# Attention into an MLP block on one core: per-head loads for the first two batches, key bias inside the score matmul, weights cast by DMA, 1/std at the output

## The chip, the core and the metric

The kernel runs on one core of one Trainium2 chip. The engines are TensorE (PE; its weight loads are shown as PEld), VectorE (DVE), ScalarE (ACT), GpSimd (POOL) and SyncE (SP, which here only issues DMAs). The metric is the device time of one execution in microseconds.

## The reference

Attention over 8 batches of 8 heads, 576 tokens, head size 64, with a bias from a running sum; then, on the concatenated heads (512 wide), a normalization, two matmuls with a ReLU between them, and a residual.

```python
scores = scale * np.matmul(q, k.transpose(0, 1, 3, 2))        # scale = 1/8
cum = np.cumsum(np.maximum(s, 0.0), axis=-1)
bias = -(cum[:, :, :, None] - cum[:, :, None, :])
scores = np.where(causal, -1000000000.0, scores + np.minimum(bias, 0.0))
attn = softmax(scores)
x = concat_heads(np.matmul(attn, v))                          # (8, 576, 512)
xn = (x - mu) / np.sqrt(var + 1e-06) * g_ln
out = x + np.maximum(xn @ w_ch1, 0.0) @ w_ch2                 # 512 -> 2048 -> 512
```

Inputs and the output are float32; the kernel's matmuls are bfloat16 with float32 sums.

## The kernel before

**Tiles.** A batch's 576 tokens are four full blocks of 128 and a tail of 64. Scores are held transposed, with keys on the partitions; only the causal part is computed, five key blocks with 576, 448, 320, 192 and 64 query columns, 1600 in all. The tile `aug` holds a batch's q and k for all heads in bfloat16, tokens on the partitions. In column 64 q carries minus the running sum and k carries a one, so the score matmul (65 rows deep) subtracts the query's sum. The key's sum is added by the bias operand of the exp, one exp for each key block (`score_exp`, L186). GpSimd then zeroes the upper triangle of the diagonal blocks. `values` (L207) multiplies with v, whose 65th column of ones gives the denominator, and DVE divides.

**Transposes.** q and k must stand with the head size on the partitions (`qkT`). For batches 0 and 1 PE transposes them head by head (`t_pe`, L150). For batches 2 to 7 DMA transposes do, one for each token block of all heads, issued by SP (`t_dma`, L157). The normalized activations are transposed by DMA too (`x_t`, L293; for chunk 0 by PE).

**The MLP.** Each batch's four full token blocks are one chunk. The tails of four batches make a half-size chunk each (chunks 8 and 9). `chunk_units` (L321) puts a chunk's work into a list of units of four 128 x 128 x 512 matmuls: 16 units up (each followed by a ReLU, ACT and DVE by turns) and 16 down (every fourth followed by the residual add); a tail chunk has 16 in all. The loop over the 64 heads takes units off this list, `n_units` a head (4 unless the table says otherwise), and sets them between the score matmuls of head g, its exps, and the values of head g-1. So the order on every engine is the order in which this loop issues work.

**Loads.** Everything comes as float32 into a staging ring of eight tiles (`stage`), loaded by SP for a token block of all eight heads (for batch 0 of four heads, `half`, L366), and is cast on DVE, ACT or POOL. A load waits until `casts` has freed a tile. The first weight is loaded in the same way in sixteen pieces and scaled by the gain in the cast (`cast_w1`, L136); the second goes through four casting DMAs issued by POOL (L500).

**Normalization.** `norm` (L263): DVE takes mean and variance, POOL computes (variance + eps) to the power -0.5, DVE subtracts and scales, a transpose and the up-matmuls follow.

**The start.** Batch 0's heads run without units. Then, at g = 8, chunk 0 is normalized, 11 units run, and batch 1 is cast and begins with one unit a head. At g = 16 ten units stand between the transposes of batch 2.

## Time and profile before

| | before |
|---|---|
| median of 3 runs | 460.45 us (458.38 to 460.86) |
| the profiled execution | 456.99 us, span 455.3 us |
| PE busy | 365.8 us (80%), 2741 matmuls |
| DVE busy | 204.1 us (45%) |
| ACT busy | 189.4 us (42%), of it exps 127.8 and 21.3 us |
| POOL busy | 148.2 us (33%) |
| mean granted PE clock | 0.908 |
| DMA moved | 64.61 MB, mean 142 GB/s; SP's queue 61.1% of the 16 engines |

A row of a busy group reads: line, engine, operation, what is written and from what, shapes, count; then busy time and mean ns of one; then the engine's idle time just before these instructions and what ended most of it. A timeline row reads: start and duration in us, engine, line, operation, tiles, count, and in brackets the idle time before it with its releaser. `SPq` rows are SP's DMA issues.

### The profile page before, as it was taken

The numbers are of one execution on the slowest core, as the hardware profiler recorded it, in microseconds if no ns is written. First come the engines' busy times: TensorE is split into PE (matmuls) and PEld (weight loads), VectorE is DVE, ScalarE is ACT, GpSimd is POOL, SyncE is SP. The second block draws the span as 40 slices with busy tenths as digits, with TensorE's granted clock in tenths as the row PEclk, the third lists the DMA queues.
The fourth block names the chain that finished last, engine by engine and source line by source line (L and its number), as shares of the span: only waits on it lengthen the run. The fifth ranks groups of instructions, "written<-read, shape, count | busy, mean of one in ns | idle before, by whom it ended". The sixth has DMA issues, their size and how long they took to land.

```text
span 455.3 us, 7530 instructions
## 1 busy us (share of the span) xinstructions
PE 365.8 (80%) x2741; PEld 198.7 (44%) x2741; DVE 204.1 (45%) x462; ACT 189.4 (42%) x408; POOL 148.2 (33%) x307
## 2 busy tenths in 40 slices
PE   1982745894074999699919999968999999999995
PEld 1751313551032555355517545534555455444472
DVE  7557233571042455353734374317436544723231
ACT  2753521760051654365405574525555644203020
POOL 4333312452143344443633365315433222100000
PEclk9996685999575999899968999979999999999999
DMA  7990699729968993999498929992992111320112
GB/s 169 205 326 20 96 212 200 150 36 225 215 144 178 207 199 96 194 209 214 112 208 177 233 65 169 219 249 48 193 205 72 31 46 48 61 80 24 48 46 46
DMA packets 202277, 64.61 MB, mean 142 GB/s; under 512 B 193472, under 2 KB 195520, under 8 KB 202240
## 3 DMA queue, kind: packets, MB, share of 16 engines
q1 hardware_dynamic: 196352, 55.22, 61.1%
q10 hardware_dynamic: 3776, 6.82, 4.4%
q0 software_dynamic: 2112, 2.10, 2.9%
q8 instruction: 21, 0.34, 0.3%
q14 instruction: 16, 0.13, 0.1%
HBM read 36.85 MB, written 9.44 MB: 102 GB/s over the span
## 4 chain that ended last, share of the span: by engine, by line
PE 57%; DVE 13%; DMA 8%; POOL 5%; issue 5%; SPq 4%; ACT 2%; DVEq 0%; POOLq 0%; ACTq 0%
PE py L345 22%; PE ph L334 22%; PE s L174 6%; PE pot L216 4%; SPq L102 3%; DVE xn L287 3%; DMA qkT<-aug 3%; DVE stats L261 3%; POOL rstd L270 2%; DVE hT L319 2%; SPq L158 2%; DVE x L226 1%; DMA xnT<-xn 1%; ACT e L192 1%; DVE yo L351 1%
## 5 line engine op out<-in xcount | busy, mean ns | idle before, releaser
L192 ACT ACTIVATE e<-s,cumk 128x576 bf16<-128x576 f32 (+3 forms) x256 | 127.8, 582 | 112.4 <-PE s L174 97.7
L334 PE MATMUL ph<-xnT,w_bf 128*128 128x512 bf16 x512 | 128.0, 396 | 14.9 <-DMA xnT<-xn 9.7
L345 PE MATMUL py<-w_bf,hT 128*128 128x512 bf16 x576 | 135.2, 382 | 0.0
L199 POOL TENSOR_SCALAR_AFFINE_SELECT e<-e 128x512 bf16<-128x512 bf16 (+1 forms) x128 | 59.5, 488 | 167.8 <-issue 93.5
L334 PEld LDWEIGHTS <-w_bf 128*128 128x128 bf16 x640 | 61.5, 102 | 82.0 <-issue 24.1
L317 ACT ACTIVATE hT<-ph 128x512 bf16<-128x512 f32 x72 | 43.4, 603 | 121.8 <-PE ph L334 115.1
L319 DVE TENSOR_SCALAR hT<-ph 128x512 bf16<-128x512 f32 x72 | 49.4, 689 | 74.6 <-PE ph L334 73.3
L345 PEld LDWEIGHTS <-hT 128*128 128x128 bf16 x576 | 53.3, 98 | 57.1 <-issue 1.7
L174 PE MATMUL s<-qkT 65*128 65x512 bf16 (+4 forms) x320 | 60.2, 320 | 21.4 <-DMA qkT<-aug 21.2
L174 PEld LDWEIGHTS <-qkT 65*128 65x128 bf16 x384 | 34.7, 105 | 62.5 <-issue 29.8
L225 DVE RECIPROCAL rinv<-pot 128x5 f32<-128x5 f32 x64 | 12.2, 191 | 91.9 <-PE pot L216 90.1
L118 POOL CAST aug<-st 128x512 bf16<-128x512 f32 (+3 forms) x65 | 39.4, 630 | 21.9 <-DMA st<-in_k_dram 21.9
L216 PEld LDWEIGHTS <-e 128*128 128x128 bf16 x960 | 39.7, 101 | 14.5 <-POOL e L199 3.0
L216 PE MATMUL pot<-v_bf,e 128*128 128x65 bf16 x960 | 42.7, 199 | 2.6 <-POOL e L199 1.8
L351 DVE TENSOR_TENSOR yo<-py,x 128x512 f32<-128x512 f32 x32 | 22.1, 690 | 26.4 <-PE py L345 25.2
L226 DVE TENSOR_TENSOR x<-pot,rinv 128x320 f32<-128x320 f32 x64 | 31.5, 492 | 2.2
L154 PE MATMUL pt<-ident,aug 128*128 128x128 bf16 x160 | 17.4, 269 | 14.1 <-DVE aug L132 11.3
L287 DVE TENSOR_SCALAR xn<-x,mv,rstd 128x512 bf16<-128x512 f32 x30 | 21.1, 740 | 16.3 <-POOL rstd L270 15.1
L334 PE MATMUL ph<-xnT_tail,w_bf 128*128 128x256 bf16 x128 | 16.5, 290 | 9.5 <-DMA xnT_tail<-xn 9.5
L118 POOL CAST v_bf<-st 128x512 bf16<-128x512 f32 (+1 forms) x35 | 20.6, 613 | 10.4 <-DMA st<-in_v_dram 10.4
L261 DVE BATCH_NORM_STATS2 stats<-x 128x6 f32<-128x256 f32 (+2 forms) x68 | 23.2, 396 | 0.0
L192 ACT ACTIVATE e<-pot,cumk 128x64 bf16<-128x64 f32 x64 | 21.3, 332 | 1.0 <-PE pot L174 1.0
(51 smaller groups left out, 128.0 us busy)
## 6 DMA issues: line engine op xcount, KB each, us to landing
st<-in_k_dram SPq DMA_DIRECT2D x28, 256.0 KB, 4.6
st<-in_v_dram SPq DMA_DIRECT2D x28, 256.0 KB, 4.1
st<-in_q_dram SPq DMA_DIRECT2D x24, 256.0 KB, 4.4
out_dram<-yo ACTq DMA_DIRECT2D x24, 256.0 KB, 3.6
hT<-in_moe_w_ch_dram SPq DMA_DIRECT2D x8, 256.0 KB, 5.7
st<-in_moe_w_ch_dram SPq DMA_DIRECT2D x8, 256.0 KB, 5.5
w_bf<-in_moe_w_ch_dram POOLq DMA_DIRECT2D x4, 512.0 KB, 10.1
out_dram<-yo SPq DMA_DIRECT2D x8, 256.0 KB, 2.0
```

Source lines behind the costliest of these rows:

```text
L118: nc.gpsimd.tensor_copy(out=o, in_=i)
L174: nc.tensor.matmul(o, lhsT=qkT[b][0:D1, H + h, kb * P : (kb + 1) * P], rhs=qkT[b][0:D1, h, lo:hi], start=True, stop=True,)
L192: nc.scalar.activation(out=e[:, kb * S : kb * S + w], in_=srcs[kb], func=ACT.Exp, bias=cumk[:, kb, g : g + 1], scale=scale,)
L199: nc.gpsimd.affine_select(out=o, in_=o, compare_op=ALU.is_ge, fill=0.0, base=0, pattern=[[0, n], [1, P]] if n > 1 else [[1, P]], channel_m ...
L216: nc.tensor.matmul(pot[:, t * D1 : (t + 1) * D1], lhsT=e[:, c : c + P], rhs=v_bfs[b % 2][:, kb, h, :], start=(kb == 0), stop=(kb == t),)
L226: nc.vector.tensor_tensor(out=xs[b][:, :, h * D : (h + 1) * D], in0=pv[:, :, 0:D], in1=rv.to_broadcast([P, NT, D]), op=ALU.mult,)
L261: nc.vector.bn_stats(out=sts[c, a][:, part, :], in_=x_of(c, a)[:, lo:hi])
L287: nc.vector.tensor_scalar(out=xn[:, j, :], in0=x_of(c, a), scalar1=mv[:, j, 0:1], scalar2=rstd[:, j : j + 1], op0=ALU.subtract, op1=ALU.mult,)
L317: nc.scalar.activation(out=o, in_=i, func=ACT.Relu)
L319: nc.vector.tensor_scalar_max(out=o, in0=i, scalar1=0.0)
L334: nc.tensor.matmul(ph[:, j * tok : (j + 1) * tok], lhsT=w1_bf[:, kd, fb * P : (fb + 1) * P], rhs=xnT[c][:, :, kd, :], start=(kd == 0), sto ...
L345: nc.tensor.matmul(st["py"], lhsT=st["h"][:, fb, a * P : (a + 1) * P], rhs=w2_bf[:, fb, :], start=(fb == 0), stop=(fb == FB - 1),)
```

## The change

1. **Loads of batches 0 and 1.** Each head's q, k and v are loaded apart, 128 partitions x 4 token blocks x 64, straight into fixed tiles (`homes`: the ring, now ten tiles, and two of the three x buffers). The tails of all heads come in one load for each of q, k, v. `cast_head` casts a head's five blocks at once, q on DVE, k and v on POOL. Batch 1 is issued at heads 5 to 7.
2. **Key bias in the matmul.** The running sum times 8 is split into three bfloat16 parts (`split`), which stand in k's columns 65 to 67 against ones in q. The score matmul is 68 rows deep, and the exps need no bias, so the blocks that lie next to each other in PSUM go in one exp: 1024, 512 and 64 columns, three a head. `shift` writes both parts; from batch 2 on POOL does it, not DVE.
3. **Weights.** Both go through casting DMAs on POOL, the first at heads 2 to 5 and the second at heads 9 to 12.
4. **1/std at the output.** The gain multiplies x minus mean. The factor 1/std is left out of xn (ReLU lets a positive factor through) and multiplies the second matmul's result in the instruction that adds the residual.
5. **Order.** The work around the heads stands in hooks (`at`). There are 2 units a head in batch 1, 32 between heads 15 and 16, 3 a head in batch 2, then 4. Chunks are added to the list at the start of a head, chunk 3 ahead of tail chunk 8. Stores are held back by one.

Core of the diff:

```diff
-    AHEAD = 8
+    AHEAD = 10
...
     def shift(b, eng):
-        eng.tensor_scalar_mul(
-            out=aug[:, :, 0:H, D], in0=cumk[:, :, b * H : (b + 1) * H], scalar1=-1.0 / scale
+        hb = slice(b * H, (b + 1) * H)
+        eng.tensor_scalar_mul(out=aug[:, :, 0:H, D], in0=cumh[:, :, hb, 0], scalar1=-1.0)
+        eng.tensor_copy(out=aug[:, :, H:HD, D1:DK], in_=cumh[:, :, hb, :])
+
+    def load_w1(c):
+        nc.gpsimd.dma_start(
+            out=w1_bf[:, :, c * Dm : (c + 1) * Dm], in_=w1_r[:, :, c * Dm : (c + 1) * Dm]
...
-            nc.scalar.activation(
-                out=e[:, kb * S : kb * S + w], in_=srcs[kb], func=ACT.Exp,
-                bias=cumk[:, kb, g : g + 1], scale=scale,
+        def ex(o, i):
+            nc.scalar.activation(out=o, in_=i, func=ACT.Exp, scale=scale)
...
+        if part == 0:
+            ex(e[:, 0:1024], s01)
+        else:
+            ex(e[:, EO[2] : EO[2] + 512], s23)
+            ex(e[:, EO[4] : EO[4] + TL], pot[:, 448:512])
...
-                nc.vector.tensor_scalar(
-                    out=xn[:, j, :], in0=x_of(c, a), scalar1=mv[:, j, 0:1],
-                    scalar2=rstd[:, j : j + 1], op0=ALU.subtract, op1=ALU.mult,
-                )
+            eng.scalar_tensor_tensor(
+                out=xn[:, j, :], in0=x_of(c, a), scalar=mv[:, j, 0:1], in1=gln_b,
+                op0=ALU.subtract, op1=ALU.mult,
+            )
+        rs = rstds[c][:, idx[0] : idx[0] + n]
+        nc.gpsimd.tensor_scalar_add(out=rs, in0=mv[:, :n, 1], scalar1=1e-6)
+        nc.gpsimd.tensor_tensor(out=rs, in0=rs, in1=nhalf[:, :n], op=ALU.pow)
...
-                nc.vector.tensor_add(out=yo, in0=st["py"], in1=x_of(c, a))
+                nc.vector.scalar_tensor_tensor(
+                    out=yo, in0=st["py"], scalar=rstds[c][:, a : a + 1], in1=x_of(c, a),
+                    op0=ALU.mult, op1=ALU.add,
+                )
...
+    def head_in(what, b, h, eng):
+        t = homes[what, b]
+        eng.dma_start(
+            out=t[:, h, 0:NF, :],
+            in_=src[what][b, h, 0 : NF * P, :].rearrange("(t p) d -> p t d", p=P),
+        )
...
+    def feed(b, h):
+        w = 1 + b
+        for j in range(3 + w * h + 1, 3 + w * h + w + 1):
+            if j < H:
+                cast_head("q", b, j, "dve")
+                cast_head("k", b, j, "pool")
+        for j in range(w * h + 1, w * h + w + 1):
+            if j < H:
+                cast_head("v", b, j, "pool")
...
+    def second_chunk():
+        values(15)
+        for i in ((0, 1), (2, 3)):
+            tiles(1, i, 1, 256, 512)
+            ready(1, i, 2)
+            mlp(2)
+        t_dma(2, 1)
+        for p in (3, 4):
+            c2(p)
+        chunk_units(1)
+        mlp(8)
+        t_dma(2, 2)
+        loads()
+        for p in range(NT):
+            casts("v", 2, p, "pool")
+            mlp(4)
+            if p < 2:
+                t_dma(2, 3 + p)
+            loads()
```

Three places in the order of the engines. First SP's DMA queue at the start of the program; `st`, `ring`, `x` are the tiles that the loads fill. Before:

```order
L91 DMA x<-in_s_dram 64x576
L370 DMA st<-in_q_dram 128x4x64
L370 DMA st<-in_k_dram 128x4x64
L370 DMA st<-in_q_dram 128x4x64
L370 DMA st<-in_k_dram 128x4x64
```

and of the change:

```order
L94 DMA x_103<-in_s_dram 64x576
L382 DMA ring<-in_q_dram 128x4x64
L382 DMA ring<-in_k_dram 128x4x64
L382 DMA ring<-in_q_dram 128x4x64
L382 DMA ring<-in_k_dram 128x4x64
L382 DMA x_104<-in_v_dram 128x4x64
```

The sizes are the same, but before a load is one token block of four heads, and all five pairs are needed for head 0; now it is four token blocks of one head, and head h needs the first h + 1 pairs.

Second ACT's queue from the exps of head 15 to those of head 16 (`e` the exps, `hT` the ReLU's output, `yo` a store). Before:

```order
L192 ACTIVATE e_111<-s_1221,cumk 128x576
L192 ACTIVATE e_111<-s_1221,cumk 128x448
L192 ACTIVATE e_111<-s_1222,cumk 128x320
L192 ACTIVATE e_111<-s_1222,cumk 128x192
L192 ACTIVATE e_111<-pot,cumk 128x64
L256 DMA out_dram<-yo 128x512 x2
L192 ACTIVATE e_112<-s_1353,cumk 128x576
```

and of the change:

```order
L188 ACTIVATE e_100<-s_1149 128x1024
L188 ACTIVATE e_100<-s_1150 128x512
L188 ACTIVATE e_100<-pot 128x64
L257 DMA out_dram<-yo 128x512 x3
L310 ACTIVATE hT<-ph 128x512 x8
L188 ACTIVATE e_101<-s_1434 128x1024
```

Eight of the sixteen ReLUs of chunk 1 (the other eight are DVE's) now stand between the two heads, so chunk 1's sixteen up-units do; before it was the rest of chunk 0's down-units alone.

Third DVE's queue at a normalization, with its waits (`mv` mean and variance, `xn` the normalized tile, `rinv` and `x` the values' division). Before:

```order
L261 BN_STATS stats<-x 128x6 x2
L267 BN_AGGR mv<-stats 128x2 [waits DVE_49] x2
L287 TENSOR_SCALAR xn<-x,mv,rstd 128x512 [waits DMAHW5_49,DVE_49,Pool_49]
L287 TENSOR_SCALAR xn<-x,mv,rstd 128x512 [waits DVE_49]
L319 TENSOR_SCALAR hT<-ph 128x512 [waits PE_49]
```

and of the change:

```order
L262 BN_STATS stats<-x_105 128x6 x2
L273 BN_AGGR mv<-stats 128x2 [waits DVE_49] x2
L277 SCALAR_TENSOR_TENSOR xn<-x_105,mv,gln_b 128x512 [waits DMAHW6_49,DVE_49]
L277 SCALAR_TENSOR_TENSOR xn<-x_105,mv,gln_b 128x512 [waits DVE_49]
L344 SCALAR_TENSOR_TENSOR yo<-py,rstd,x_103 128x512 [waits DMAHW4_49,PE_49]
```

The wait for POOL is gone from the normalization.

More of the change, by code (lines that the diff above doesn't have):

```diff
@@ L45 @@
     D1 = D + 1
+    DK = D + 4
     BH = B * H
@@ L441, with loads, casts @@
-    for p in range(NT):
-        dma_in(v0[:, p, :], src_of(v, 0, p))
-        staged["v", 0, p] = v0[:, p, :]
+    def loads():
+        while n_loaded[0] < len(seq) and room[0] > 0:
+            key = seq[n_loaded[0]]
+            t = ring[:, n_loaded[0] % AHEAD, :]
+            room[0] -= 1
+            dma_in(t, src_of(src[key[0]], key[1], key[2]), nc.sync)
+            staged[key] = t
+            n_loaded[0] += 1
+    def casts(what, b, p, eng):
+        cast((what, b, p), eng)
+        room[0] += 1
@@ L444 @@
+    for what in "qkv":
+        tails_in(what, 0, nc.scalar)
+    for h in range(H + 1):
+        if h < H:
+            head_in("q", 0, h, nc.sync)
+            head_in("k", 0, h, nc.sync)
+        if h:
+            head_in("v", 0, h - 1, nc.sync)
     nc.vector.memset(ones, 1.0)
+    nc.vector.memset(cum[:, S:SP_], 0.0)
     nc.vector.memset(nhalf, -0.5)
-    nc.vector.memset(cum[:, S:SP_], 0.0)
-    nc.vector.memset(aug[:, :, :, D1:P], 0.0)
-    nc.gpsimd.memset(aug[64:P, NF, :, 0:D], 0.0)
@@ new lines, in t1, with c1, first_chunk @@
+    def t1(h):
+        t_pe(1, h, ("dve", "act"))
+    def c1(h):
+        cast_head("q", 1, h, "dve")
+        cast_head("k", 1, h, "pool")
+    def first_chunk():
+        values(7)
+        for a in range(NF):
+            stats(0, a, 2, 448, 512)
+        for i in ((0, 1), (2, 3)):
+            norm(0, i, 3)
+            x_t(0, i, pe=True)
+        chunk_units(0)
+        new_t(1)
+        c1(0)
+        shift(1, nc.vector)
+        mlp(1)
+        t1(0)
+        c1(1)
+        mlp(1)
+        t1(1)
+        cast_head("v", 1, 0, "pool")
+        c1(2)
+        c1(3)
@@ L534 @@
-        if b == 0:
-            for i in early.get(g, ()):
-                t_pe(0, i)
-        if b == 1 and h + 2 < H:
-            t_pe(b, h + 2)
-        if 1 <= g <= NG and g != 8:
+        run(g, "b")
+        if 1 <= g <= NG and g not in (8, 16):
             values(g - 1)
-        if g == 7:
-            values(7)
+        run(g, "x")
+        run(g, "c")
         mlp(min(1, nu - 2))
-        if g < NG and h == 5:
-            for a in range(NF):
-                stats(b, a, 0, 0, 256)
```

411 lines of the change are left out of this document (183 added, 228 removed).

## The prediction

> **What bounds the kernel now.** I read the page first: the span, the busy tenths of TensorE (PE) in 40 slices of 11.4 us, and the chain that ended last by line.
>
> ```profile
> span 455.3 us, 7530 instructions
> ...
> PE   1982745894074999699919999968999999999995
> ...
> PE py L345 22%; PE ph L334 22%; PE s L174 6%; PE pot L216 4%; SPq L102 3%; DVE xn L287 3%; DMA qkT<-aug 3%; DVE stats L261 3%; POOL rstd L270 2%; DVE hT L319 2%; SPq L158 2%; DVE x L226 1%; DMA xnT<-xn 1%; ACT e L192 1%; DVE yo L351 1%
> ```
>
> The chain is mostly the two MLP matmuls, so PE bounds the whole. But the slices show PE full only from slice 14 on. Ahead of it lie holes (slices 4, 6 to 7, 10 to 11, 13). Their causes stand in the timeline of PE: start, duration, instructions, and in brackets the idle time before with what ended it.
>
> ```profile
> 12.40 1.49 PE L174 MATMUL s<-qkT 65*128 65x512 bf16 x5
> ...
> 38.24 1.01 PE L216 MATMUL pot<-v_bf,e 128*128 128x65 bf16 x15 [1.46 <-POOL e L199]
> ...
> 50.44 11.53 PE L334 MATMUL ph<-xnT,w_bf 128*128 128x512 bf16 x44 [0.67 <-ACT xnT L114]
> 73.31 1.94 PE L154 MATMUL pt<-ident,aug 128*128 128x128 bf16 x14 [11.34 <-DVE aug L132]
> ...
> 120.94 0.58 PE L174 MATMUL s<-qkT 65*128 65x512 bf16 x1 [13.02 <-DMA qkT<-aug]
> 125.75 1.01 PE L174 MATMUL s<-qkT 65*128 65x64 bf16 x4 [4.22 <-DMA qkT<-aug]
> ```
>
> Batch 0 (heads 0 to 7) runs from 12.40 to 39.25. The normalization of chunk 0 lasts until 50.44. Eleven units (a unit is four matmuls of 512 columns) later PE waits for batch 1's q and k to be loaded and cast, until 73.31. After head 15 it waits for the DMA transposes of batch 2, until 125.75. From head 18 on four units stand beside each head:
>
> ```profile
> 187.49 1.89 PE L334 MATMUL ph<-xnT,w_bf 128*128 128x512 bf16 x4 [3.79 <-DMA xnT<-xn]
> 189.17 1.49 PE L174 MATMUL s<-qkT 65*128 65x512 bf16 x5
> ...
> 222.13 0.82 PE L174 MATMUL s<-qkT 65*128 65x512 bf16 x5
> 237.42 1.87 PE L334 MATMUL ph<-xnT_tail,w_bf 128*128 128x256 bf16 x8 [9.46 <-DMA xnT_tail<-xn]
> ...
> 245.14 0.82 PE L174 MATMUL s<-qkT 65*128 65x512 bf16 x5
> 268.38 1.02 PE L334 MATMUL ph<-xnT,w_bf 128*128 128x512 bf16 x4 [0.93 <-DVE hT L319]
> 279.25 0.82 PE L174 MATMUL s<-qkT 65*128 65x512 bf16 x5
> 297.62 0.38 PE L174 MATMUL s<-qkT 65*128 65x512 bf16 x1
> 301.91 1.01 PE L174 MATMUL s<-qkT 65*128 65x64 bf16 x4 [3.91 <-DMA qkT<-aug]
> 375.74 0.82 PE L174 MATMUL s<-qkT 65*128 65x512 bf16 x5
> ```
>
> Heads 27, 34, 37, 44, 48 and 63 start at 189.17, 222.13, 245.14, 279.25, 297.62 and 375.74. Undisturbed, a head takes (297.62 - 279.25) / 4 = 4.59 us. Heads 27 to 63 take 186.6 us where 36 x 4.59 = 165.3 would do: 21.3 us are stalls, 9.2 of them at 222 to 245.
>
> **The change part by part.** I carry the sum along marks on PE's line.
>
> *Mark 1, the end of head 7.* The start needs only head 0's q and k. The rate of the loads is seen where ACT waits for them, two 128 KB loads (q and k) per cast:
>
> ```profile
> 4.80 0.41 ACT L114 CAST aug<-st 128x256 bf16<-128x256 f32 x1 [2.72 <-DMA st<-in_k_dram]
> 8.45 0.41 ACT L114 CAST aug<-st 128x256 bf16<-128x256 f32 x1 [0.76 <-DMA st<-in_k_dram]
> ```
>
> The first and the fourth lie 3.65 us apart: six loads, 0.6 us each. Three loads a head (the same 128 KB) are 1.8 us a head. With three tail loads ahead, head 0 lands near 6 and the k of head 7 near 19. The key path (scan, transposes, now five VectorE (DVE) steps where one was, two shifts where one was) is 2 us longer, and a long memset ahead of it is shorter by as much, so the first score comes at 10 to 12. Each head also casts the q and k of a head four further on, and these casts stand in DVE's and POOL's order ahead of this head's copies and masks; so the first four heads go at the pace of the loads, 1.8 us each plus a first wait, to about 21. Then the head's own work decides. ACT now does three exps for five:
>
> ```profile
> L192 ACT ACTIVATE e<-s,cumk 128x576 bf16<-128x576 f32 x64 | 47.4, 741 | 112.4 <-PE s L174 97.7 <-DVE stats L261 10.9 <-PE pot L174 3.0
> L192 ACT ACTIVATE e<-pot,cumk 128x64 bf16<-128x64 f32 x64 | 21.3, 332 | 1.0 <-PE pot L174 1.0
> L317 ACT ACTIVATE hT<-ph 128x512 bf16<-128x512 f32 x72 | 43.4, 603 | 121.8 <-PE ph L334 115.1 <-PE s L174 4.3 <-PE pot L174 2.3
> L118 POOL CAST v_bf<-st 128x512 bf16<-128x512 f32 (+1 forms) x35 | 20.6, 613 | 10.4 <-DMA st<-in_v_dram 10.4
> ...
> L500 POOL DMA_DIRECT2D w_bf<-in_moe_w_ch_dram x4 | 3.3, 832 | 0.0
> ...
> 82.56 0.87 POOL L199 TENSOR_SCALAR_AFFINE_SELECT e<-e 128x512 bf16<-128x512 bf16 x2
> ```
>
> The exp rows differ by 409 ns over 512 elements: 0.80 ns each and 281 ns fixed. Five exps of 1600 elements are 2.69 us, three 2.12; without a bias operand, as in the ReLU row (603 ns for 512, so 193 fixed), 1.86. I take 1.9, near the ReLU row. POOL has 0.87 of masks, two casts of 320 elements (estimated at 0.45 each from the 613 ns of 512) and at four heads a weight DMA of 0.83, so 1.8 to 2.6. Four heads at 2.5 with the last values end near 33: **6 us less**. Bounds: 29 if only ACT counted (2.0 a head), 39.25 if loads and POOL eat it all. The three key-bias rows make the score matmul 68 rows deep for 65. I cost that at nothing: five matmuls 65 deep take 0.82 us for 1536 columns (222.13 above), eight 128 deep 1.73 for 4096 (a row below), so depth does not cost.
>
> *Mark 2, the first up-matmul.* The chain that ended last, in order of time, shows what fills the 11.2 us after head 7, and at its end the price of a unit.
>
> ```profile
> 40.08 1.93 DVE w_bf L142 x4
> 42.01 1.55 DVE stats L261 x8
> ...
> 44.19 0.73 POOL rstd L270
> ...
> 150.65 1.73 PE ph L334 x8
> ```
>
> The four weight casts (1.93) are gone, the longer half of the stats (0.8) moves ahead of head 7's values, and POOL's rstd chain (0.73 and an add before it, 1.0 with the way there and back), which came twice, is no longer waited for. 11.2 - 1.93 - 0.8 - 2.0 = 6.5, and the first up-matmul comes at 39.5 against 50.44. Bound: 8 if the new normalization is slower.
>
> *Mark 3, head 16.* Two units run, then batch 1 begins, whose loads were issued at heads 5 to 7 and lie beside the casting weight DMAs. They were not visible before, so bounds: head 8 starts at 43 if all has landed; if the 7.7 MB of both go at the 210 GB/s that the second hole of before shows below, from 17 on, the last lands at 54 and heads 9 and 10 wait 3 to 4. I take 45. Each of eight heads now carries two units of 0.87 (1.73 / 2). A head without units is 4.59 - 4 x 0.87 = 1.1, ten transposes 0.6, waits as before 0.3: 3.75 x 8 = 30, so head 15 ends at 75. Then 32 units stand ahead of head 16 where 10 or 11 stood, 28 us. Beside them SP issues two xnT transposes and four qkT transposes:
>
> ```profile
> 185.60 3.46 SPq L158 DMA_TRANSPOSE qkT<-aug  x1
> ...
> 204.97 4.11 SPq L158 DMA_TRANSPOSE qkT<-aug  x1
> ...
> qkT<-aug SPq DMA_TRANSPOSE x30, 5.8
> xnT<-xn SPq DMA_TRANSPOSE x14, 3.1
> ```
>
> Four intervals between those five, with the loads among them, are 19.4 us: 4.85 each. Chain, two xnT and four at 4.85 end near 75 + 9 + 19 = 103, landing a little later; the units end at 104. **Head 16 at 105**, against 125.75; 50 units are done by then, not 28.
>
> *Mark 4, head 27.* Here cover is gone. 14 units are left for heads 16 to 20, and heads 21 to 25 have none, since chunk 2 comes at head 26. PE could do heads 16 to 23 in 14 x 0.87 + 8 x 1.4 = 23 us. But SP must transpose batch 3 between the cast at head 16 and head 24: start 110.5, fifth issue 19.4 later, landing 5.8 later: 136. So the queue of transposes ends last, not PE. Then two short heads, the normalization of chunk 2 and its xnT (3.1): first unit at 147.5 (187.49 before), three more units, **head 27 at 152.5** against 189.17. Bounds: 145 if the transposes go closer together, 158 if they queue behind loads.
>
> *Mark 5, head 63.* Of the 21.3 us of stalls some go. The DVE chain of a normalization:
>
> ```profile
> 265.62 1.56 DVE L287 TENSOR_SCALAR xn<-x,mv,rstd 128x512 bf16<-128x512 f32 x2 [1.14 <-POOL rstd L270]
> ...
> 267.11 0.70 DVE L132 TENSOR_SCALAR aug<-cumk 128x40 bf16<-128x40 f32 x1
> ```
>
> The wait of 1.14 goes and the shift of 0.70 moves to POOL, more than the 0.93 that PE stalled. The tail chunk's 9.46 goes, since its units now queue behind chunk 3's; but chunk 3 is itself late by the same path as the 3.79 at 187.49, so 4.6 of 9.2 stay. The 3.91 wait for qkT at head 48 (some 6 with the cold clock after it) I halve: two more ring buffers, the same transposes. Left: 4.6 + 3 + 2.4 of small ones = 10, between 5 and 25. Head 63 at 152.5 + 165.3 + 10 = 328.
>
> *The end.* Before: 455.3 - 375.7 = 79.6. The order has seven units more done by head 63, so 73.5. The output step is as long as the add it replaces. Span 401.5.
>
> The profiled execution of before took 456.99 us for a span of 455.3, 1.7 around it: **403**. The median of the runs of before, 460.45, is 3.5 over that, so I move to **404**.
>
> A rule against the change: "SBUF — State Buffer" of the Trainium skill, section Who interferes with whom, says that a VectorE instruction with two SBUF inputs blocks against a GpSimd instruction reading SBUF. The new normalization has two (x and the gain), the old one had one. By that rule each pair could lose up to one POOL cast of 0.65, 14 pairs in the steady part, 9 us at most; the sum would then be 413. The row above, 1.56 for two, is the old form beside POOL's casts; I take the new one as no longer, so I add nothing.
>
> **The rivals.**
>
> *The transposes bind throughout.* SP's queue is late at every batch as at head 48: three or four more stalls of 4 to 6 us, and batch 1's casts wait. 404 + 12 to 24: **416 to 428**. For it: the 13.02 and the 3.91; against: a batch of eight heads has 36.7 us and its five transposes take 24.
>
> *They do not bind.* Heads 16 to 24 run at PE's 23 us and stall 48 goes: **388 to 393**.
>
> *PE's clock stays low: slower than before.* The place is the start up to head 27, where PE would now be half busy instead of idle in long holes.
>
> ```profile
> 38.00:42.00 4.00, 1.01 (x15) 0.85 (x15) 2.83 (x8) 0.00 (x0) 1.23 (x3) 0.50 0.01 2
> 62.00:74.00 12.00, 0.69 (x7) 0.69 (x8) 2.05 (x6) 0.60 (x1) 2.58 (x5) 0.60 1.27 210
> 90.00:94.00 4.00, 3.46 (x52) 2.50 (x53) 2.31 (x6) 3.22 (x8) 1.31 (x4) 1.00 0.02 4
> ```
>
> These rows by stretch give PE busy second and, third from the end, the granted clock (then DMA share, GB/s). A quarter busy goes with 0.50, 3.46 of 4 with 1.00. The stretch to head 27 holds 68 units and 27 heads, 59 + 30 + 9 of transposes = 98 us at full clock. At half clock all through it would be 98 more: **502**. It is slower than before once over 55 of the 98 run at half. Against it: batch 1 with one unit a head already held 1.00. The Trainium skill, "TensorE: Matmul & The Clock Gate", part 1, has this as a rule: half rate is the default, and about 3.4 us of sustained work release it; the trace agrees with 0.50 after idle stretches.
>
> *The loads do not come earlier.* The per-head loads only move the wait: marks 1 to 3 each keep their holes, and the gain is what DVE's chain and marks 4 and 5 give, 15 to 20: **438 to 443**.
>
> **How the numbers follow.** Forecast (394 to 414) 0.50; transposes bind 0.22; do not bind 0.18; loads not earlier 0.06; clock 0.03; several losses that cancel the gain, near 457, 0.01. The range 388 to 428 takes the first three with their bounds. A measurement of this kernel can tell about 0.5% from no change; faster by more 0.96, within 0.01, slower 0.03.
>
> **What would show it.** Right: head 7 ends by 35, no PE hole over 5 us before head 16, which starts at 100 to 110; a wait for qkT at head 24 and for xnT at head 26; no DVE wait for POOL ahead of xn; head 27 to 63 in 170 to 180. Wrong: heads 8 to 10 waiting for casts of q or k by over 5 us, a clock of 0.5 between heads 8 and 16, or new qkT waits at heads 32, 40 and 56.

## The result and the profile after

The changed kernel took **402.75 us** (median of four runs, 400.46 to 403.41), the kernel before, run beside it on the same chip, 459.56 us (458.38 to 460.86). The ratio is **0.8754**, with a 95% interval of 0.8707 to 0.8802. The prediction was 404 us, and its range of 388 to 428 holds the time. Below, a median takes in all four runs of a kernel, but its ratio leaves out slow executions: one with 1/std ahead (median of the other three 413.72) and two with the activations transposed by PE (median of the other two 395.84).

The page of the changed kernel, with the same parts as before: span, TensorE (PE) by slices (now 10.0 us each), granted clock, chain by line.

```profile
span 401.4 us, 7323 instructions
...
PE   2775899999996439996999999799999999999995
...
PEclk9996799999996559999799999999999999999999
...
PE ph L327 30%; PE py L338 27%; PE s L171 7%; PE pot L218 5%; DMA qkT<-aug 5%; DMA ring<-in_q_dram 2%; DMA x<-in_q_dram 2%; SPq L382 2%; DMA out_dram<-yo 2%; DMA xnT<-xn 2%; PE pt L151 2%; DVE x L227 1%; DVE xn L277 1%; SPq L155 1%; DVE stats L262 1%
```

PE is now full from slice 6 to slice 12. Behind them one deep hole is left, slices 13 to 15 (120 to 150 us), and shallow ones at slices 19 and 26. The two MLP matmuls hold 57% of the chain instead of 44%; ScalarE's (ACT's) exps and GpSimd's (POOL's) rstd are gone from the part of it that is shown.

The timeline of PE at the marks of the prediction (start, duration, instructions, idle time before and what ended it):

```profile
10.29 1.46 PE L171 MATMUL s<-qkT 68*128 68x512 bf16 x5 [0.78 <-ACT qkT L111]
...
33.51 1.01 PE L218 MATMUL pot<-v_bf,e 128*128 128x65 bf16 x15 [0.43 <-POOL e L191]
...
40.85 1.86 PE L327 MATMUL ph<-xnT,w_bf 128*128 128x512 bf16 x4 [0.68 <-ACT xnT L111]
...
46.13 0.82 PE L171 MATMUL s<-qkT 68*128 68x512 bf16 x5
...
103.30 0.89 PE L171 MATMUL s<-qkT 68*128 68x512 bf16 x5
...
131.30 0.59 PE L171 MATMUL s<-qkT 68*128 68x512 bf16 x1 [2.13 <-issue]
136.27 1.01 PE L171 MATMUL s<-qkT 68*128 68x64 bf16 x4 [4.38 <-DMA qkT<-aug]
...
148.48 3.46 PE L327 MATMUL ph<-xnT,w_bf 128*128 128x512 bf16 x8 [6.22 <-DMA xnT<-xn]
...
153.97 0.82 PE L171 MATMUL s<-qkT 68*128 68x512 bf16 x5
...
191.01 3.59 PE L327 MATMUL ph<-xnT,w_bf 128*128 128x512 bf16 x8 [4.04 <-DMA xnT<-xn]
...
329.24 0.82 PE L171 MATMUL s<-qkT 68*128 68x512 bf16 x5
```

These rows, beside those of before and the forecast, in us from the start of the span:

| mark | before | forecast | after | gain so far |
|---|---|---|---|---|
| first score | 12.40 | 10 to 12 | 10.29 | 2.1 |
| end of head 7's values | 39.25 | 33 | 34.52 | 4.7 |
| first up-matmul | 50.44 | 39.5 | 40.85 | 9.6 |
| head 16 | 120.94, rest at 125.75 | 105 | 103.30 | 17.6 to 22.5 |
| first unit of chunk 2 | 187.49 | 147.5 | 148.48 | 39.0 |
| head 27 | 189.17 | 152.5 | 153.97 | 35.2 |
| head 63 | 375.74 | 328 | 329.24 | 46.5 |
| end of the span | 455.3 | 401.5 | 401.4 | 53.9 |

So two thirds of the gain (35.2 of 53.9) are made by head 27, before PE is full for good. Heads 27 to 63 give 11.3 and the end 7.4.

### The profile page after: what moved, and what is told of

Its sections match the earlier page's. It is cut to its first block, busy times and chain, and to the rows that moved or that the text cites. A ratio compares the mean times of both kernels' runs of the same rounds, so it can differ in the third digit from the quotient of the medians.

```text
span 401.4 us, 7323 instructions
## 1 busy us (share of the span) xinstructions
PE 353.1 (88%) x2717; PEld 195.0 (49%) x2741; DVE 195.7 (49%) x454; ACT 156.3 (39%) x278; POOL 169.4 (42%) x325
## 4 chain that ended last, share of the span: by engine, by line
PE 72%; DMA 13%; DVE 6%; SPq 4%; issue 2%; ACT 1%; POOL 0%; ACTq 0%; DVEq 0%
PE ph L327 30%; PE py L338 27%; PE s L171 7%; PE pot L218 5%; DMA qkT<-aug 5%; DMA ring<-in_q_dram 2%; DMA x<-in_q_dram 2%; SPq L382 2%; DMA out_dram<-yo 2%; DMA xnT<-xn 2%; PE pt L151 2%; DVE x L227 1%; DVE xn L277 1%; SPq L155 1%; DVE stats L262 1%
## 5 line engine op out<-in xcount | busy, mean ns | idle before, releaser
L188 ACT ACTIVATE e<-s 128x1024 bf16<-128x1024 f32 (+1 forms) x128 | 99.9, 809 | 102.1 <-PE s L171 93.2
L191 POOL TENSOR_SCALAR_AFFINE_SELECT e<-e 128x384 bf16<-128x384 bf16 (+1 forms) x128 | 57.7, 474 | 115.5 <-ACT e L188 104.7
L171 PE MATMUL s<-qkT 68*128 68x512 bf16 (+4 forms) x320 | 57.5, 310 | 10.0 <-DMA qkT<-aug 6.3
L171 PEld LDWEIGHTS <-qkT 68*128 68x128 bf16 x384 | 33.3, 101 | 50.2 <-issue 14.0
L344 DVE SCALAR_TENSOR_TENSOR yo<-py,rstd,x 128x512 f32<-128x512 f32 x32 | 24.0, 749 | 41.7 <-PE py L338 35.6
L115 POOL CAST aug<-ring 128x512 bf16<-128x512 f32 (+2 forms) x71 | 39.3, 575 | 8.8 <-DMA ring<-in_k_dram 8.7
L277 DVE SCALAR_TENSOR_TENSOR xn<-x,mv,gln_b 128x512 bf16<-128x512 f32 x32 | 22.7, 752 | 0.0
L115 POOL CAST v_bf<-ring 128x512 bf16<-128x512 f32 (+2 forms) x38 | 21.1, 582 | 0.0
L283 POOL TENSOR_TENSOR rstd<-rstd,nhalf 128x2 f32<-128x2 f32 x18 | 19.2, 1067 | 1.5
L151 PE MATMUL pt<-ident,aug 128*68 128x128 bf16 x160 | 14.7, 252 | 3.7 <-DVE aug L130 1.6
```

The costliest lines, as they stand in the source:

```text
L115: nc.gpsimd.tensor_copy(out=o, in_=i)
L171: nc.tensor.matmul(o, lhsT=qkT[b][0:DK, H + h, kb * P : (kb + 1) * P], rhs=qkT[b][0:DK, h, lo:hi], start=True, stop=True,)
L188: nc.scalar.activation(out=o, in_=i, func=ACT.Exp, scale=scale)
L191: nc.gpsimd.affine_select(out=d, in_=d, compare_op=ALU.is_ge, fill=0.0, base=0, pattern=[[0, d.shape[1]], [1, P]], channel_multiplier=-1,)
L277: eng.scalar_tensor_tensor(out=xn[:, j, :], in0=x_of(c, a), scalar=mv[:, j, 0:1], in1=gln_b, op0=ALU.subtract, op1=ALU.mult,)
```

## The experiments

Each kernel below ran with a profile and three more timings beside the kernel before on the same chip. Spans and marks are of the one profiled execution of each kernel, while a ratio rests on several runs. Equal work differs a little too: the runs of the changed kernel have spans of 398.4 to 401.4, and head 7's values end between 33.72 and 35.60 in seven profiled kernels (the changed one among them) that are the same up to there. Ratios are to the kernel before. Unless said otherwise an edit is made in the changed kernel, whose span is 401.4 and whose ratio 0.8754.

### Loads by token block

The first two batches are loaded a token block of all eight heads at a time, into the same tiles. For batch 0 this is coarser than in the kernel before, which loaded four heads at a time.

```diff
+    def block_in(what, b, p, eng):
+        t = homes[what, b]
+        eng.dma_start(
+            out=t[:, :, p, :],
+            in_=src[what][b, :, p * P : (p + 1) * P, :].rearrange("h s d -> s h d"),
...
-    for h in range(H + 1):
-        if h < H:
-            head_in("q", 0, h, nc.sync)
-            head_in("k", 0, h, nc.sync)
-        if h:
-            head_in("v", 0, h - 1, nc.sync)
+    for p in range(NF):
+        block_in("q", 0, p, nc.sync)
+        block_in("k", 0, p, nc.sync)
+    for p in range(NF):
+        block_in("v", 0, p, nc.sync)
...
```

> Undone: the per-head loads. Batches 0 and 1 come in token blocks of all eight heads (256 KB each), into the same tiles, with the same casts. Theory (the early start feeds the line of marks): head 0 needs all eight q and k blocks, so its score comes at 15 to 17 instead of 10.3, head 7 ends at 36 to 38 instead of 34.5, and head 8 waits 2 to 4 us more: 4 to 8 us slower than the changed kernel, about 407 to 411. Rival (the first eight heads are paced by their own work and by VectorE, so a later start is caught up and only the order of the units matters): under 2 us slower, 403 to 405.

Measured: span 409.7, median 411.87, ratio 0.898 (0.892 to 0.904). VectorE (DVE) shows where it starts, and PE what follows, in two timelines:

```profile
14.59 0.48 DVE L113 CAST aug<-ring 128x320 bf16<-128x320 f32 x1 [8.82 <-DMA ring<-in_q_dram]
```

```profile
18.82 1.46 PE L171 MATMUL s<-qkT 68*128 68x512 bf16 x5 [0.78 <-DVE aug L113]
```

DVE waits 8.82 for q, and the first score moves from 10.29 to 18.82, 8.5 later. Head 7 starts 6.9 later (37.56 after 30.65), so 1.6 are made good by then. Head 8, whose q and k now come by block too, starts 9.6 later (55.71 after 46.13). The span is 8.3 longer: the later start reaches the end. But 8.3 is not what the change gained by its loads, since the kernel before, with blocks of four heads, had its first score at 12.40 and not at 18.82.

### 1/std ahead of the normalization

The normalization multiplies with 1/std as before, and so waits for POOL; the output step is an add. The gain is left out.

```diff
-            eng.scalar_tensor_tensor(
-                out=xn[:, j, :], in0=x_of(c, a), scalar=mv[:, j, 0:1], in1=gln_b,
-                op0=ALU.subtract, op1=ALU.mult,
...
+            nc.vector.tensor_scalar(
+                out=xn[:, j, :], in0=x_of(c, a), scalar1=mv[:, j, 0:1],
+                scalar2=rs[:, j : j + 1], op0=ALU.subtract, op1=ALU.mult,
...
+                nc.vector.tensor_add(out=yo, in0=st["py"], in1=x_of(c, a))
```

> Undone: 1/std at the output. VectorE's normalization waits for GpSimd's rstd again and multiplies with it; the output step only adds. The gain is left out of the computation. Theory: 2 us more ahead of the first up-matmul, 1 to 2 us more at each of the chunk starts at heads 26 and 34, 0.5 to 1 us at each of the two normalizations of the later batches: 5 to 9 us slower than the changed kernel, 408 to 412. Rival (the wait is hidden behind other stalls): under 2 us, 403 to 405.

Measured: span 410.3, median 416.09, ratio 0.905 (0.8962 to 0.9138). DVE's timeline at chunk 2:

```profile
141.58 1.56 DVE L279 TENSOR_SCALAR xn<-x,mv,rstd 128x512 bf16<-128x512 f32 x2 [1.16 <-POOL rstd L276]
```

and PE's at chunk 3:

```profile
195.30 3.60 PE L326 MATMUL ph<-xnT,w_bf 128*128 128x512 bf16 x8 [5.82 <-DMA xnT<-xn]
```

Each pair of tiles waits 1.1 to 1.2 for POOL again. Chunk 2's first unit comes 2.3 later (150.75 after 148.48), and heads 27 to 63 take 180.9 where 175.3 did. Of these 5.6, 1.8 stand at chunk 3's first unit (a wait of 5.82 after 4.04) and 2.4 at head 40 (a wait for `qkT` of 2.88 after 0.50). The first is behind a normalization that waits for POOL; whether the second belongs to it is not shown, since this wait is 2.11 with the late units below, whose normalization is the changed kernel's.

### Five exps a head

The exps stay without bias, but go block by block.

```diff
-            ex(e[:, 0:1024], s01)
+            ex(e[:, 0:S], s01[:, 0:S])
+            ex(e[:, S:1024], s01[:, S:1024])
...
-            ex(e[:, EO[2] : EO[2] + 512], s23)
+            ex(e[:, EO[2] : EO[2] + 320], s23[:, 0:320])
+            ex(e[:, EO[3] : EO[3] + 192], s23[:, 320:512])
```

> Undone: the merging of the exps. Five exps a head again, by key block, still without a bias operand. Theory (ScalarE is not the bound except in heads without units): about 0.4 us more work a head on ScalarE, of which only the eight heads of batch 0 feel a part: 0 to 3 us slower, 403 to 406. Rival (the shorter exps carry the steady part): 37 heads at 0.2 to 0.4, 7 to 15 us slower, 410 to 418.

Measured: span 400.5, median 401.70, ratio 0.8753 (0.8686 to 0.8819): no cost. In the changed kernel a head's exps are the three groups

```profile
L188 ACT ACTIVATE e<-s 128x1024 bf16<-128x1024 f32 x64 | 65.6, 1025 | 101.2 <-PE s L171 93.2 <-POOL aug L115 3.7 <-POOL e L191 2.3
L188 ACT ACTIVATE e<-s 128x512 bf16<-128x512 f32 x64 | 38.0, 594 | 0.9 <-issue 0.9
L188 ACT ACTIVATE e<-pot 128x64 bf16<-128x64 f32 x64 | 14.9, 232 | 2.6 <-PE pot L171 2.6
```

of 1.85 us together (the forecast had 1.9), and ACT idled 101.2 us ahead of the first, most of it for PE's scores. ACT does not bind even where heads have no units: heads 3 to 6 follow each other at 2.1 with three exps and with five. So merging the exps brought no time that these runs can tell. What the score matmul's key bias brings by itself was not tried, since these exps have no bias operand either. "ScalarE: Activation LUTs" of the Trainium skill, section What ACT_TABLE_LOAD costs, gives 186 ns and 0.833 ns an element for an immediate scale and bias, by which the estimates are 1039, 612 and 239 ns. The rows agree within about 3%.

### Chunk 1's units after head 16, not ahead of it

Only 14 units stand between heads 15 and 16 instead of 32; all 32 units of chunk 1 follow with heads 18 to 25, four a head.

```diff
-        chunk_units(1)
         mlp(8)
         t_dma(2, 2)
...
+    at(18, "a", lambda: chunk_units(1))
...
-    n_units = {8: 2, 9: 2, 10: 2, 11: 2, 12: 2, 13: 2, 14: 2, 15: 2, 16: 3, 17: 3, 18: 3, 19: 3, 20: 3, 21: 3, 22: 3, 23: 3}
+    n_units = {8: 2, 9: 2, 10: 2, 11: 2, 12: 2, 13: 2, 14: 2, 15: 2, 16: 3, 17: 3}
```

> Undone: the early units of chunk 1. They join the list at head 18, as before the change, four a head; 14 units stand between heads 15 and 16 where 32 stood. Theory (the queue of transposes ends last from head 15 to head 24, so the place of the units inside this stretch is nearly free): TensorE idles from 88 to 103 and head 16 comes where it came, heads 18 to 25 take 4.6 each, the first unit of chunk 2 comes 2 to 5 us later: 405 to 408. Rival (the filled hole between heads 15 and 16 is the gain): 18 units of 0.87 come back in full, 14 to 16 us slower, 417 to 419.

Measured: span 401.3, median 403.47, ratio 0.8822 (0.8758 to 0.8886). PE's timeline:

```profile
98.78 0.59 PE L171 MATMUL s<-qkT 68*128 68x512 bf16 x1 [11.62 <-DMA qkT<-aug]
102.49 1.01 PE L171 MATMUL s<-qkT 68*128 68x64 bf16 x4 [3.13 <-DMA qkT<-aug]
```

The old hole is back, 14.75 us of it, and costs little or nothing: the profiled span is 0.1 shorter, and the ratio is 0.7 points (3 us) higher, with intervals that overlap. The rival's 14 to 16 us are far off. Head 16's last score matmuls start at 102.49, and in the changed kernel all five start at 103.30: the transposes end there whatever PE does meanwhile. And the units that were not done then are done beside heads 18 to 25, in time that PE otherwise spends waiting for batch 3's transposes (head 24 starts at 135.54; its last score matmuls stood at 136.27). Chunk 2's first unit comes 1.0 later (149.52), not the 2 to 5 of the theory. The 18 units moved ahead of head 16 fill a hole, but by themselves they bring no time that these runs can tell.

### Batch 2's casts two heads later

Casts of batch 2's q and k at heads 14 and 15 instead of 12 to 14, and its first transpose at head 15 instead of 13.

```diff
-        for p in (3, 4):
+        for p in (2, 3, 4):
             c2(p)
...
-        at(12 + p, "d", lambda p=p: c2(p))
-    at(13, "d", lambda: t_dma(2, 0))
+        if p < 2:
+            at(14 + p, "d", lambda p=p: c2(p))
+    at(15, "d", lambda: t_dma(2, 0))
```

> Undone: the early casts and transposes of batch 2. Its first token blocks are cast at heads 14 and 15 and the rest behind head 15, and the first DMA transpose is issued at head 15 instead of 13, as before the change; the 32 units between heads 15 and 16 stay. Theory (from head 15 to head 24 the chain of casts, DMA transposes and loads on SP is the line, and its start sets all that follows): one transpose and its loads more behind head 15, all later marks slip by 4 to 7 us: 407 to 410. Rival (the 32 units hide it, as TensorE is the line there): head 16 at 103 and no change, 402 to 404.

Measured: span 404.0, median 406.81, ratio 0.888 (0.8843 to 0.8917). The first transpose is issued at 75.51 after 68.42. Head 16's last score matmuls start at 109.20, 5.9 later; head 24's at 140.3, 4.0 later; head 27 starts 4.3 later and head 63 2.7 later. In this execution 1.7 us are made good between heads 27 and 63 by shorter waits, and the span is 2.6 longer. The medians are 4.1 apart and the ratios 1.3 points, 5.8 us, with intervals that do not touch. So the direction is the theory's, and the size lies at or near its 4 to 7.

### Batch 3 transposed by PE

PE does batch 3's transposes at heads 19 to 22; SyncE's (SP's) queue has none of them. The casts of its q and k move to heads 16 to 18.

```diff
-            at(g0 + p, "d", lambda b=b, p=p: (casts("q", b, p, "pool"), casts("k", b, p, "pool")))
-            at(g0 + p + 1, "c", lambda b=b, p=p: t_dma(b, p))
+            at(g0 + (p // 2 if b == 3 else p), "d",
+               lambda b=b, p=p: (casts("q", b, p, "pool"), casts("k", b, p, "pool")))
+            if b > 3:
+                at(g0 + p + 1, "c", lambda b=b, p=p: t_dma(b, p))
...
+        at(19 + h // 2, "c" if h % 2 else "a2", lambda h=h: t_pe(3, h, ("dve", "act")))
```

> Batch 3 is transposed by TensorE at heads 19 to 22 (its q and k cast at heads 16 to 18) instead of by five DMA transposes. Theory (the DMA transposes end last between heads 16 and 24): head 24 comes at 130 to 133 instead of 136 and later marks keep 3 to 5 us of it: 397 to 400. Rival (the line there is the heads' own work or the normalization of chunk 2): within 1.5 us of the changed kernel, 401 to 404.

Measured: span 399.5, median 401.31, ratio 0.8753 (0.8721 to 0.8786). PE's timeline:

```profile
132.04 0.86 PE L171 MATMUL s<-qkT 68*128 68x512 bf16 x5 [0.30 <-ACT e L188]
...
143.97 3.57 PE L327 MATMUL ph<-xnT,w_bf 128*128 128x512 bf16 x8 [5.92 <-DMA xnT<-xn]
```

Head 24 no longer waits for its `qkT` (0.30 for ACT), chunk 2 starts 4.5 earlier, head 27 4.3. So SP's transposes of batch 3 did set that stretch. But the wait for chunk 2's activations stays (5.92), a wait of 2.39 appears at 256, and at the end 1.9 are left, which the ratio cannot tell from nothing. The marks are the theory's; the median of 401.31 lies in the range of the rival.

### The activations of chunks 2 and 3 transposed by PE

PE transposes the normalized activations of chunks 2 and 3 behind the scores of heads 26 and 34; the later chunks keep their DMA transposes.

```diff
-                at(g0 + j, "x", lambda b=b, i=i: (tiles(b, i, 1, 256, 512), ready(b, i, 2)))
+                if b > 3:
+                    at(g0 + j, "x", lambda b=b, i=i: (tiles(b, i, 1, 256, 512), ready(b, i, 2)))
+                else:
+                    at(g0 + j, "x", lambda b=b, i=i: (tiles(b, i, 1, 256, 512), norm(b, i, 2)))
+                    at(g0 + 2, "a2", lambda b=b, i=i: x_t(b, i, pe=True))
```

> The normalized activations of chunks 2 and 3 are transposed by TensorE, behind the scores of heads 26 and 34, instead of by DMA. Theory (the first unit of a chunk waits 6.2 and 4.0 us for the DMA transpose): the waits fall to 3 to 4 and 1 to 2 us, 3 to 5 us less in all: 397 to 400. Rival (the normalization on VectorE is the wait, whoever transposes): within 1.5 us, 401 to 404.

Measured: span 393.2, median 399.35, ratio 0.8637 (0.86 to 0.8674). PE's timeline at the two chunks' first units:

```profile
143.83 3.42 PE L327 MATMUL ph<-xnT,w_bf 128*128 128x512 bf16 x8 [0.67 <-ACT xnT L111]
...
184.72 1.89 PE L327 MATMUL ph<-xnT,w_bf 128*128 128x512 bf16 x8 [0.71 <-ACT xnT L111]
```

Head 27 is 4.7 earlier (149.28), head 35 8.7 (188.63 after 197.37), head 63 8.6. Where the changed kernel waited 6.22 and 4.04 for the DMA transposes, PE now waits 0.67 and 0.71 for ACT's copy of its own transposes. The theory had 3 to 5; it was too low, since 4.7 are gained at the first chunk and 4.0 at the second.

### Both: the fastest version

The two edits above in one kernel.

> Both: batch 3's q and k and the activations of chunks 2 and 3 are transposed by TensorE. Theory: the two gains add, 6 to 10 us less than the changed kernel, 393 to 397. Rival (they shorten the same wait): no better than the better of the two alone.

Measured: span 391.6, median **392.07** (390.21 to 393.6), ratio **0.8553** (0.8518 to 0.8588). That is 2.7% under the changed kernel's median (392.07 / 402.75), or 2.3% by the two ratios, whose intervals do not touch. In the profiled spans the gains of 1.9 and 8.2 come to 9.8 together, as the theory has it, and the median is 0.9 under its 393 to 397. The rival falls, since the interval lies below that of the better single edit. Its page:

```profile
PE   2775899999999889998999999799999999999995
...
PE 79%; DVE 8%; DMA 6%; ACT 3%; issue 2%; SPq 1%; POOL 0%; DVEq 0%; ACTq 0%
```

The deep hole of slices 13 to 15 is filled, and PE holds 79% of the chain (72% in the changed kernel).

### The first weight by casting DMA in the kernel before

The kernel before, with the first weight through four casting DMAs on POOL instead of sixteen staged loads and scaled casts. The gain is left out.

```diff
-    for c in (2, 3):
-        for kd in range(KD):
-            add(("w1", kd, c), w1_r[:, kd, c * Dm : (c + 1) * Dm], (7.6, 7.7)[c - 2])
...
+        if g in (2, 3, 4, 5):
+            nc.gpsimd.dma_start(
+                out=w1_bf[:, :, (g - 2) * Dm : (g - 1) * Dm],
+                in_=w1_r[:, :, (g - 2) * Dm : (g - 1) * Dm],
...
-        if g in (6, 7):
-            for kd in range(KD):
-                cast_w1(kd, g - 6, "dve")
```

> The kernel before with one part of the change alone: the first weight comes through four casting DMAs at heads 2 to 5, so its sixteen loads leave SP and the staging ring and its sixteen casts leave VectorE and ScalarE, and batch 1's loads follow batch 0's at once. The gain is left out of the computation. Theory (the second hole of before, 62 to 73, is the weight's pieces holding the ring, so that batch 1 is loaded late): its transposes start at 58 to 62 instead of 73.3 and the later marks keep it: 11 to 15 us less than the kernel before, a ratio of 0.967 to 0.976. Rival (the next hole, the wait for batch 2's transposes at head 16, takes it back): under 4 us, a ratio over 0.99.

Measured: span 446.6, median 447.79, ratio 0.9747 (0.9665 to 0.983). PE's timeline:

```profile
48.74 10.79 PE L334 MATMUL ph<-xnT,w_bf 128*128 128x512 bf16 x44 [0.67 <-ACT xnT L114]
61.30 1.47 PE L154 MATMUL pt<-ident,aug 128*128 128x128 bf16 x20 [1.77 <-DVE aug L132]
...
107.86 0.59 PE L174 MATMUL s<-qkT 65*128 65x512 bf16 x1 [13.34 <-DMA qkT<-aug]
112.91 1.01 PE L174 MATMUL s<-qkT 65*128 65x64 bf16 x4 [4.46 <-DMA qkT<-aug]
```

The hole of 11.34 ahead of batch 1 is 1.77: in the kernel before, batch 1's q and k wait behind the sixteen float32 loads of the weight, 4 MB in all. The first up-matmul comes 1.7 earlier, without the weight casts on DVE, and heads 8 to 27 come 11.9 to 14.2 earlier. The hole at head 16 stays as large as it was (13.34 and 4.46), and 3.5 of the gain are lost again between heads 27 and 63. The batch's transposes at 61.30 and the ratio are inside the theory's ranges; the rival's ratio of over 0.99 falls.

### Four parts undone together

Loads by token block, 1/std ahead, late casts and late units, all in one kernel; the gain is left out.

> The changed kernel with four parts undone together: loads by token block, VectorE's normalization behind rstd (the gain left out), batch 2's late casts, and chunk 1's units late. Alone they cost 8.3, 8.9, 2.6 and nothing in the spans. Theory (they lie one behind another on one line): the sum, within 4 us: a span of 417 to 425. Rival (each is covered by another, the late units above all): together more than the sum, over 428, or less, under 415.

Measured: span 431.7, median 432.68, ratio 0.9445 (0.9382 to 0.9507). In the profiled spans the four cost 8.3, 8.9, 2.6 and 0 alone, 19.8 in all, and 30.3 together, the "more than the sum" of the rival. PE's timeline:

```profile
117.12 0.59 PE L171 MATMUL s<-qkT 68*128 68x512 bf16 x1 [17.76 <-DMA qkT<-aug]
121.17 1.01 PE L171 MATMUL s<-qkT 68*128 68x64 bf16 x4 [3.46 <-DMA qkT<-aug]
```

The wait ahead of head 16 is 21.2 where the late units alone had 14.75. Up to head 16 the delays add: its last score matmuls start 17.9 later than in the changed kernel, and the single delays there sum to 17.3. Head 24 is 18.7 later, where they sum to 11.8. But each of these numbers is of one execution. By the ratios, which rest on three or four runs each, the single costs are 2.26, 2.96, 1.26 and 0.68 points of the time before, 7.16 in all, and the joint cost is 6.91. So the runs do not show that the parts cover for one another: the joint cost may as well be the plain sum, as the theory has it.

### Late casts with late units

The two edits of those names together, to see whether this pair costs more than its parts.

> Two parts undone together: batch 2's casts and transposes late, and chunk 1's units late. Alone they put head 27 at 158.3 and 155.1 (153.97 in the changed kernel). Theory (the units were free only because the transposes of batch 3 left slack behind head 16; with head 16 late, the heads' four units each become the line): head 27 at 163 to 167, a span of 408 to 413. Rival (the excess of the four comes from the loads or the normalization): head 27 at 158 to 160, a span of 402 to 405.

Measured: span 405.1, median 408.61, ratio 0.8916 (0.8872 to 0.896). Head 27 is at 159.09, 5.1 later than in the changed kernel, where late casts alone had 4.3. PE waits 15.04 and 2.80 ahead of head 16, but the pair costs 3.7 in the span, against 2.6 of its parts, and 1.62 points by the ratios, against 1.94. The theory falls: the pair costs no more than its parts, within what these runs can tell.

## Why the prediction was right, step by step

**Mark 1 (head 7 ends at 33; measured 34.52).** The steps hold: the first score comes at 10.29, and DVE waits for q of heads 2 and 3 at the loads' pace, 1.80 apart as put. The miss is there by head 4, which starts at 22.84 where the first four heads were to end at about 21. Behind it a head takes 2.10, not 2.5, and this pays for a term that the sum did not have, `split` for the other seven batches: five DVE steps from 25.85 to 28.76. That the last four heads come to 11.7 where 12 was put is luck. DVE's and PE's timelines (the last row is PE's):

```profile
11.68 0.49 DVE L113 CAST aug<-ring 128x320 bf16<-128x320 f32 x1 [1.33 <-DMA ring<-in_q_dram]
13.48 0.49 DVE L113 CAST aug<-ring 128x320 bf16<-128x320 f32 x1 [1.32 <-DMA ring<-in_q_dram]
...
25.85 0.44 DVE L452 TENSOR_SCALAR xt<-pc 128x280 f32<-128x280 f32 x1
...
28.13 0.63 DVE L461 TENSOR_TENSOR cumh<-xt,cumh 128x280 bf16<-128x280 f32 x1
```

```profile
30.16 0.20 PE L171 MATMUL pot<-qkT 68*128 68x64 bf16 x1 [2.29 <-DVE x L227]
```

PE waits 2.29 behind them, for a division that stood behind the split, where heads 3 to 5 wait 0.23. With block loads head 7's values end at 41.42, 6.9 later, so the first wait does set this mark.

**Mark 2 (6.5 us from there to the first up-matmul; measured 6.33).** Right, and one term was tested: with the wait for POOL's rstd put back, head 7's values end at 34.11 and the first up-matmul comes at 42.36, 8.25 later. So this wait, put at 2.0, costs 1.9.

**Mark 3 (head 8 at 45, head 16 at 105; measured 46.13 and 103.30).** The forecast let the units and SP's transposes end together, at 104 and 103. They do, which is luck, and it hid that one of them alone decides. The late units and the late casts show which: without 18 of the units head 16's last score matmuls still start at 102.49, and with later transposes they start at 109.20. SP's queue, start and duration of the issues:

```profile
68.42 7.53 SPq L155 DMA_TRANSPOSE qkT<-aug  x1
...
83.78 7.47 SPq L155 DMA_TRANSPOSE qkT<-aug  x2
94.65 3.66 SPq L155 DMA_TRANSPOSE qkT<-aug  x1
98.99 3.00 SPq L155 DMA_TRANSPOSE qkT<-aug  x1
108.25 3.42 SPq L155 DMA_TRANSPOSE qkT<-aug  x1
...
130.84 3.52 SPq L155 DMA_TRANSPOSE qkT<-aug  x1
```

The fifth transpose of batch 2 is issued until 101.99.

**Mark 4 (head 24 at 136 by SP's queue, not PE; chunk 2 at 147.5, head 27 at 152.5; measured 136.27, 148.48, 153.97).** The named reason is the one: batch 3's transposes go from 108.25 to 130.84 and the last lands 5.4 later. The start was 2.3 earlier than the 110.5 forecast and the four intervals 22.6 instead of 19.4, which nearly cancel, by luck. The experiment with batch 3 on PE takes this wait away and moves head 27 by 4.3. Not forecast was a wait at head 20, of 4.62 on DVE for a store (the output buffer's last store took 7.30 to land):

```profile
122.59 0.75 DVE L344 SCALAR_TENSOR_TENSOR yo<-py,rstd,x 128x512 f32<-128x512 f32 x1 [4.62 <-DMA out_dram<-yo]
```

PE waited 2.50 for the division behind it, and the page's chain runs through this store. But SP's issues follow one another from 119.17 to 130.84 with gaps of at most 0.10, so as far as the rows show it was the queue that ended last, and the wait lay under the cover of the transposes.

**Mark 5 (10 of stalls left between heads 27 and 63, 175.5 in all; measured 175.27).** Of the single terms, chunk 3's wait of 4.6 measured 4.04, and the tail chunk's 9.46 is gone, both as written. The waits for `qkT` were 0.50 and 1.45 where 3 was put, so the small ones are 4.0 where 2.4 was put: the sum is right, and its last two terms, off by 1 and 1.6, cancel by luck. The 0.50 stands at head 40, one of the three heads whose new waits were to be a sign of being wrong; heads 32 and 56 have none. The removed 1.14 wait of DVE was undervalued when it was set against "the 0.93 that PE stalled": undone, these heads take 5.6 longer, in one execution and with 2.4 of it at a wait whose link is not shown.

**The end** took 72.2 where 73.5 was put. One reading of the page was loose: PE is not full from slice 14 on in the kernel before, since slices 17, 21 and 27 show 6, 1 and 6. Mark 5 counts the waits behind them.

**The rivals.** That the transposes bind throughout falls: after head 24 PE waits for `qkT` twice, 1.95 us in all. That they do not bind at all falls by the 4.38 at head 24; a kernel that has PE do those of batch 3 and of two chunks reaches the 388 to 393 of this rival (392.07). That the clock stays low falls by the windows of the changed kernel (stretch, length, busy time of PE, PEld, DVE, ACT and POOL, granted clock, DMA share, GB/s):

```profile
34.00:46.00 12.00, 8.10 (x52) 4.84 (x50) 7.49 (x24) 3.63 (x6) 7.49 (x14) 0.51 1.23 222
46.00:72.00 26.00, 24.36 (x257) 14.83 (x255) 15.90 (x38) 19.51 (x35) 14.99 (x31) 1.00 1.08 189
72.00:104.00 32.00, 31.45 (x174) 14.69 (x174) 16.18 (x34) 6.42 (x11) 10.19 (x19) 1.00 1.10 213
104.00:136.00 32.00, 23.15 (x205) 13.27 (x206) 9.02 (x22) 13.15 (x24) 15.86 (x33) 0.82 1.14 208
136.00:154.00 18.00, 11.14 (x79) 5.98 (x79) 7.43 (x19) 6.08 (x11) 10.76 (x19) 0.56 1.07 197
```

From head 8 to 16 it is 1.00; low clocks stand only beside the holes that are left. That the loads are not earlier falls by the first marks (the first score at 10.29 after 12.40, head 7's end at 34.52 after 39.25). The block loads show the price of a later start, but not of the start of before, as their first score comes 6.4 later than that.

**What stays open.** Of the 53.9 us, undoing four parts takes back 30.3, but one of them, the loads, is undone further than it was before, so 30.3 is likely more than these four parts brought. The casting DMAs alone gave the kernel before 8.7. The two come from different kernels and are not to be added. What is left over was not taken apart: the key bias in the score matmul, chunk 3 ahead of the tail chunk (the tail chunk's wait of 9.46 is gone, but no run puts the old order back), the ring of ten tiles and the fixed tiles, the hooks' order, and the shift on POOL.

## What to carry to other kernels

Where a hole in the bounding engine is ended by a queue of DMA transposes, ask what ends it before filling it: here 18 units moved into the hole brought no time that the runs could tell, an earlier first transpose did, and so did taking the transposes of two chunks off that queue. Value a part of a change by undoing it alone and with its neighbours, and by several runs of each: here the profiled spans gave 19.8 for the single costs and 30.3 for the joint one, and the ratios of three or four runs each 7.16 and 6.91 points. Undo a part to what stood there before; a part undone further looks larger than it was. A sum that comes out right may hold terms that cancel, so the marks along the way are worth forecasting and reading one by one.

## What was not expected of the hardware

A POOL power of 128 x 2 elements takes longer where DVE's new normalization runs beside it. The groups of the kernel before, of the kernel with 1/std ahead, and of the changed one:

```profile
L270 POOL TENSOR_TENSOR rstd<-rstd,nhalf 128x2 f32<-128x2 f32 x18 | 12.8, 714 | 1.5
```

```profile
L276 POOL TENSOR_TENSOR rstd<-rstd,nhalf 128x2 f32<-128x2 f32 x18 | 12.9, 717 | 1.5
```

```profile
L283 POOL TENSOR_TENSOR rstd<-rstd,nhalf 128x2 f32<-128x2 f32 x18 | 19.2, 1067 | 1.5
...
L277 DVE SCALAR_TENSOR_TENSOR xn<-x,mv,gln_b 128x512 bf16<-128x512 f32 x32 | 22.7, 752 | 0.0
```

Its mean is 1067 ns after 714, and 717 again where DVE waits for it, so the cause lies in the normalization or the output step, the two things that this run puts back. The changed kernel itself shows both lengths, in POOL's timeline:

```profile
140.84 1.07 POOL L283 TENSOR_TENSOR rstd<-rstd,nhalf 128x2 f32<-128x2 f32 x1
...
145.18 0.73 POOL L283 TENSOR_TENSOR rstd<-rstd,nhalf 128x2 f32<-128x2 f32 x1
```

Of the 18 powers this second one alone has no DVE instruction beside it, and it takes 0.73; the other 17 run for some 0.5 us beside a normalization and take 1.07 to 1.20. DVE pays little: its new normalization takes 752 ns, where the old form took 740 in the kernel before and 706 with 1/std ahead. "SBUF — State Buffer" of the Trainium skill, section Who interferes with whom, says that a DVE instruction with two SBUF inputs contends with a GpSimd instruction that reads SBUF. The rows agree, with POOL as the one that pays; the loss on DVE's side that the prediction put at up to 9 us by that rule did not come. That the port named there is the cause was not isolated by a run.
